# Turning activations by transfer instead of by matrix multiply: attention output and first expert tiles of a linear attention and mixture-of-experts kernel on one core

## Chip, core and metric

The kernel runs as one program on one core of a Trainium2 chip. The core's five engines work side by side and meet through semaphores: TensorE (PE; its weight loads are shown apart as PEld), VectorE (DVE), ScalarE (ACT), GpSimd (POOL) and SyncE (SP), which here only issues transfers. The metric is the device time of one execution in microseconds (us), the median over runs. A "turn" below is the transposition of a 128-row tile, so that its columns come to lie on the partitions and it can be the contracted operand of a matrix multiply.

## What is computed

Three stages follow one another: a linear attention with a decaying state over 4 x 8 heads of 768 steps and width 48; a dense two-layer block with a leaky ReLU; and a mixture of 8 experts, of which each token takes the one with the largest logit.

```python
# _attn_ref: per batch b, head h, step t
state = alpha[:, :, t, :, None] * state + np.einsum('bhd,bhe->bhde', k[:, :, t], v[:, :, t])
y[:, :, t] = np.einsum('bhd,bhde->bhe', q[:, :, t], state)
x = attn_out.transpose(0, 2, 1, 3).reshape(3072, 384)
# _moe_ref: w_in is 384 x 2048, w_out is 2048 x 384
h = x @ w_in
x = np.maximum(0.01 * h, h) @ w_out
# _moe2_ref: w1 is 8 x 384 x 1024, w2 is 8 x 1024 x 384
logits = x @ w_gate
expert_idx = np.argmax(logits, axis=1)
gate_w = softmax(logits)[np.arange(N), expert_idx]
for e in range(8):
    mask = expert_idx == e
    out[mask] = gate_w[mask, None] * (np.maximum(x[mask] @ w1[e], 0.0) @ w2[e])
```

## The kernel before

The 3072 tokens are worked in 8 **units** of 384 (NU = 8), each of three chunks of 128. Attention runs by chunks (scores, then the sum with the running state), with the decays folded into the keys and queries by VectorE scans. Precision is kept by splitting numbers into a float16 high and low part; each product is then three matrix multiplies (high-high, high-low, low-high).

**Attention's output** of a chunk is made in `chunk` (lines 693 to 789). The product stands in PSUM; VectorE finds its largest magnitude (L763) and a power of two (`pow2`, L537 to L542), ScalarE scales it into a float32 tile `xh` (L767), TensorE turns its three 128 x 128 blocks against an identity (L777 for units 2 to 7, L775 for units 0 and 1), ScalarE copies the turned high part to `xT` (L781) and VectorE subtracts to get the low part (L789). `xT` has two buffers.

**The dense block** is `moe1`: for each unit 16 groups of 9 multiplies against `w_in` (L825), whose results pass through `leaky` (ScalarE L802, VectorE L804, ScalarE L807, then GpSimd L809), and three sums of 48 multiplies against `w_out` (L834). `finish` scales the result to a float16 pair `xg` (L880 to L895). `route` computes logits, the chosen expert and each token's place in a list by experts in HBM (`x2s`), and GpSimd scatters the rows there (L967).

**The order** of all this is not written out: generators (`chunk`, `moe1`, `route` and so on) yield operations with an engine, an estimated duration, needs and rings of buffers, and the class `Loom` lists them by estimated start and by priority. The estimates set only the order. Transfers (engine "D") are issued on SP's queue, which works strictly in that order; low halves of weights are also loaded in between (`ck`, L531) and checked by VectorE (L533).

**The experts** work on 26 tiles of 128 gathered rows, four times (phases; each takes a quarter of the 1024 hidden columns). The first NA = 14 tiles hold full tiles of units 0 to 6, so that they can be gathered (`gather`, L1198, on GpSimd) while unit 7 is still in `moe1`. `tile_gathers` and `tile_turns` do as much of this as fits inside the Loom; `experts` goes on with the rest, one gather for each tile (L1490 ff.). `turn` transposes a gathered tile by six float16 blocks on TensorE (L1212), and a ScalarE copy (L1214) puts the result into `XT`. For each tile `experts` issues the 18 multiplies of `hidden` (L1334), the next gather, the copy of the expert's first weights (`stage`, L1251), ReLU parts (L1342, L1346), pieces of the next phase's weights, and the 6 multiplies of `combine` (L1363) of the tile two before. `last_tiles` runs beside the first tiles: the last unit's `route` with its three scatters, then `second_table`, then the 12 gathers of the remaining tiles. The expert number of a tile is read from `ej` into a register by `reg` (L1220) on VectorE, on TensorE and, for split tiles, on ScalarE; each read is followed by a check of its bounds.

## Time and profile before

| | us |
|---|---|
| median of 3 runs (768.33 to 771.94) | 769.94 |
| profiled execution, time | 772.55 |
| profiled execution, span from first to last instruction | 770.8 |
| TensorE busy in it (7927 multiplies) | 745.1 |
| VectorE / ScalarE / GpSimd busy | 607.2 / 483.0 / 378.7 |

Read the busy times against the span first, and then, stage by stage, which wait ends last on the engine that is busy nearly all the time; a timeline row shows in square brackets how long the engine sat idle before it and what released it. Matrix multiplies are pipelined and overlap in the rows, so the step from one start to the next, not the duration of a row, is what a multiply costs.

### The profile page before, as it was taken

What the parts mean: (1) busy time and instruction counts of PE and PEld (TensorE: products, weight loads), DVE (VectorE), ACT (ScalarE), POOL (GpSimd) and SP (SyncE); (2) the same over time, 40 slices, a digit from 0 to 9 for tenths busy, and PEclk for the clock granted to TensorE, in tenths of its full rate; (3) what the DMA queues carried; (4) which work ended last, traced back from release to release, by engine and by line L of the source; (5) the groups of instructions that cost most, each with busy time, mean ns of one, the idle gap of its engine ahead of it and who ended that gap; (6) DMA issues with size and microseconds to landing.
All of it is one profiled execution on the core that took longest, in us unless ns stands there. A gap on an engine that the chain in (4) does not pass through costs nothing.

```text
span 770.8 us, 21013 instructions
## 1 busy us (share of the span) xinstructions
PE 745.1 (97%) x7927; PEld 509.1 (66%) x7927; DVE 607.2 (79%) x1435; ACT 483.0 (63%) x1083; POOL 378.7 (49%) x406
## 2 busy tenths in 40 slices
PE   9999999998999999999999999899999999999994
PEld 4656675665666666656766665557777777777773
DVE  8999986599799879759855547756878899888673
ACT  4877576789866856845864645824676566667530
POOL 9135024451742763571581270553442588786543
PEclk9999999999999999999999999999999999999998
DMA  9914331153436234223001225224287555653341
GB/s 365 372 55 123 125 125 59 61 168 124 158 100 222 73 102 167 84 83 123 3 21 32 63 70 162 78 83 130 93 280 244 169 170 164 192 185 122 130 178 69
DMA packets 53131, 102.67 MB, mean 133 GB/s; under 512 B 4893, under 2 KB 37715, under 8 KB 53024
## 3 DMA queue, kind: packets, MB, share of 16 engines
q1 hardware_dynamic: 39360, 74.03, 29.9%
q0 software_dynamic: 4960, 14.62, 5.5%
q10 hardware_dynamic: 8704, 12.58, 4.8%
q8 instruction: 67, 1.10, 0.6%
q14 instruction: 40, 0.33, 0.1%
HBM read 79.17 MB, written 9.86 MB: 115 GB/s over the span
## 4 chain that ended last, share of the span: by engine, by line
PE 80%; DVE 11%; DMA 3%; issue 2%; ACT 2%; POOL 1%; ACTq 0%; DVEq 0%; POOLq 0%
PE m L834 22%; PE m L825 21%; PE a L1334 12%; PE m L1363 11%; PE a L710 3%; PE m L390 2%; PE a L754 2%; DMA wr<-in_moe_w 2%; PE a L669 1%; PE a L741 1%; PE a L637 1%; DVE st L1251 1%; DVE w L417 1%; DVE w L419 1%; PE a L486 1%
## 5 line engine op out<-in xcount | busy, mean ns | idle before, releaser
L834 PE MATMUL m<-woh,gh 128*128 128x392 f16 x1152 | 201.8, 329 | 0.0
L825 PE MATMUL m<-xT,wih 128*128 128x384 f16 x1152 | 193.8, 326 | 2.5 <-DVE gf L804 2.5
L809 POOL TENSOR_TENSOR gh<-gf,gh 128x384 f16<-128x384 f32 x128 | 119.0, 940 | 132.6 <-ACT gh L807 129.1
L825 PEld LDWEIGHTS <-wih 128*128 128x128 f16 x1152 | 111.8, 98 | 76.0 <-issue 4.7
L834 PEld LDWEIGHTS <-gh 128*128 128x128 f16 x1152 | 110.3, 98 | 73.4 <-issue 1.4
L1363 PE MATMUL m<-W,hs 128*128 (+1 forms) x624 | 119.1, 326 | 3.2 <-issue 1.8
L1334 PE MATMUL a<-XT,st 128*128 128x128 f16 (+1 forms) x1872 | 117.3, 215 | 3.0 <-DVE st L1251 1.6
L1334 PEld LDWEIGHTS <-st 128*128 128x128 f16 x1872 | 105.9, 98 | 21.0 <-issue 4.7
L804 DVE SCALAR_TENSOR_TENSOR gf<-m,gf 128x384 f32<-128x384 f32 x128 | 70.1, 554 | 55.6 <-ACT gf L802 55.4
L1251 DVE COPY st<-W 128x1536 f16 x104 | 82.7, 795 | 27.4 <-PE a L1334 16.2
L802 ACT ACTIVATE gf<-m 128x384 f32<-128x384 f32 x128 | 62.3, 489 | 42.9 <-PE m L825 39.1
L1342 ACT ACTIVATE hs<-a 128x256 f16<-128x256 f32 x104 | 39.7, 383 | 73.6 <-PE a L1334 52.8
L1363 PEld LDWEIGHTS <-hs 128*128 128x128 f16 (+1 forms) x720 | 57.6, 101 | 32.4 <-issue 3.0
L807 ACT CAST gh<-gf 128x384 f16<-128x384 f32 x128 | 64.4, 507 | 7.4 <-DVE gf L804 7.2
L1133 POOL TENSOR_TENSOR W<-wr,W 128x768 f16<-128x768 f32 x32 | 57.2, 1790 | 7.7 <-ACT W L1132 7.7
L1198 POOL DMA_INDIRECT acc<-x_rows,offj x26 | 30.3, 1164 | 37.3 <-DVE offj L1195 28.4
L1346 DVE SCALAR_TENSOR_TENSOR hs<-a,hs 128x256 f16<-128x256 f32 x104 | 43.2, 415 | 6.1 <-ACT hs L1342 5.4
L1106 POOL TENSOR_SCALAR wr<-wr 128x768 f32<-128x768 f32 x32 | 30.5, 952 | 27.7 <-DMA wr<-in_moe_w 14.9
L351 ACT ACTIVATE scrap<-W 128x768 bf16<-128x768 f16 x48 | 40.2, 838 | 5.9 <-ACT hs L1342 5.5
L1384 POOL DMA_INDIRECT out<-acc x26 | 26.5, 1019 | 31.7 <-DVE acc L1381 20.9
L967 POOL DMA_INDIRECT x_rows<-xg,pi x24 | 25.7, 1071 | 24.7 <-issue 6.4
L728 POOL TENSOR_TENSOR sh<-sm,sh 128x512 f16<-128x512 f32 x17 | 23.4, 1387 | 27.1 <-ACT sh L723 27.1
(279 smaller groups left out, 1238.6 us busy)
## 6 DMA issues: line engine op xcount, KB each, us to landing
wr<-in_moe_w SPq DMA_DIRECT2D x64, 384.0 KB
so<-W ACTq DMA_DIRECT2D x32, 384.0 KB
al<-in_aT SPq DMA_DIRECT2D x16, 390.0 KB
raw_in<-in_moe_w_in SPq DMA_DIRECT2D x12, 512.0 KB
kn__125<-in_kT SPq DMA_DIRECT2D x8, 768.0 KB
qn__126<-in_qT SPq DMA_DIRECT2D x8, 768.0 KB
raw<-in_moe_w_out SPq DMA_DIRECT2D x16, 384.0 KB
ck<-in_moe_w_in SPq DMA_DIRECT2D x24, 256.0 KB
```

Of the source, the lines that this page charges most:

```text
L351: A.activation(scrap, src, AF.Square, scale=scale, accum_out=g_sq[:, i : i + 1])
L802: A.activation(gf, ph[:, 0:UT], AF.Copy, scale=0.01 * CG)
L804: V.scalar_tensor_tensor(gf, ph[:, 0:UT], CG, gf, ALU.mult, ALU.max)
L807: A.copy(gh[:, 0], gf)
L809: E_[e].tensor_tensor(out=gh[:, 1], in0=gf, in1=gh[:, 0], op=ALU.subtract)
L825: T.matmul(ph[:, 0:UT], wih[:, a, kk, f * P : (f + 1) * P], xT[:, b, kk, :], start=(n == 0), stop=(n == 8),)
L834: T.matmul(po[:, 0:ROW], g[f][:, a, c * P : (c + 1) * P], woh_[0][:, b, f, :], start=(n == 0), stop=(n == 3 * NF - 1),)
L1133: G.tensor_tensor(out=lo, in0=raw, in1=hi, op=ALU.subtract)
L1251: V.tensor_copy(out=sth[i % 2].rearrange("p a k f -> p a (k f)"), in_=Wp[ph][0][:, :, ds(reg(V, j), 1), :, :].rearrange("p a e k f -> p a ...
L1334: T.matmul(hp[:, f * P + z * w : f * P + (z + 1) * w], st[z][:, a, kk, f * P : (f + 1) * P], XT[j][:, b, kk, z * w : (z + 1) * w], start=( ...
L1346: V.scalar_tensor_tensor(hs[:, 1].rearrange("p i t -> p (i t)"), hp[:, 0 : 2 * P], 0.0, hs[:, 0].rearrange("p i t -> p (i t)"), ALU.max, A ...
L1363: T.matmul(yp[z * w : (z + 1) * w, 0:DM], hs[:, a, i, z * w : (z + 1) * w], w2, start=(n == 0), stop=(n == 5), skip_group_check=True,)
```

## The change

Five things change.

- In `chunk`, units 2 to 7: ScalarE writes the scaled output as float16 (high part) straight into the first half of `xh`, VectorE writes the low part from PSUM into the second half (L772 of the new kernel), and one transfer on SP's queue (L778) turns all six blocks into `xT`. The three multiplies (L777), the copy (L781) and the subtraction (L789) of these 18 chunks go.
- `tile_turns` (L1250 of the new kernel) turns the tiles that are gathered inside the Loom by a transfer in place of six multiplies and a copy. In the built order these are five tiles; the other 21 are turned on TensorE as before.
- The last unit's scatters are declared free of the 14 first gathers (group "full"), so that they no longer wait for these to land.
- `experts` issues two first gathers instead of one in each of its first two tiles, and `last_tiles` loses one empty step.
- `reg` loads without the check of bounds.

Two estimates of the Loom change with it: when a buffer that a transfer reads comes free, and a lag in `route`; they only move the order.

```diff
         for name, key in op.free:
-            self.rings[name].drop(key, t)
+            self.rings[name].drop(key, t + (4.0 if last == "D" else 0.0))
...
+        if half:
+            yield O("A", 0.62)
+            x16 = pa.tile([P, DM], F32, tag="xh", name="xh", bufs=2).bitcast(F16)
+            A.activation(x16[:, 0:DM], yp[:, 0:DM], AF.Copy, scale=s1)
+            yield O("V", 0.62, free=[YA, ("n1", (u, c))])
+            V.scalar_tensor_tensor(
+                x16[:, DM : 2 * DM], yp[:, 0:DM], s1, x16[:, 0:DM], ALU.mult, ALU.subtract
+            )
+            yield O("D", 1.0, take=[("xT", u)], free=[("xh", (u, c))], post=[("xT", u, c)])
+            if r["xT"] is None:
+                r["xT"] = pm.tile([P, 2, 3, UT], F16, tag="xT", name="xT", bufs=2)
+            nc.sync.dma_start_transpose(out=r["xT"][:, :, :, sl].rearrange("p a k t -> p (a k) t"), in_=x16)
+            return
...
-                T.transpose(o, t, ident)
...
-            yield O("V", 0.58, free=[XA], post=[("xT", u, c)])
-            V.tensor_tensor(out=xT[:, 1, :, sl], in0=pxv, in1=xT[:, 0, :, sl], op=ALU.subtract)
...
-        yield O("v", 1.65, post=[("cu", u)], lag=1.0)
+        yield O("v", 1.65, post=[("cu", u)], lag=2.0 if u < NU - 2 else 1.0)
...
             tc.add_to_no_dep_group("list", sc.ins)
+            if last:
+                tc.declare_no_dep(sc.ins, group="full", reason="full tiles hold no row of the last unit")
...
+        if j < NA:
+            tc.add_to_no_dep_group("full", ga.ins)
...
-            regs[eng, j, z] = eng.value_load(ej[HALF * z : HALF * z + 1, j : j + 1], min_val=0, max_val=E - 1)
+            regs[eng, j, z] = nc.values_load(
+                ej[HALF * z : HALF * z + 1, j : j + 1], engines=(eng.engine,), min_val=0, max_val=E - 1,
+                skip_runtime_bounds_check_because="both tables hold 0 to E - 1 alone",
+            )
...
         for j in range(NA):
-            yield O("PA", (0.4, 0.75), need=[("acc", j)], take=[("a", ("t", j))], free=[("a", ("t", j))])
-            turn(j)()
+            yield O("D", 1.25, need=[("acc", j)])
+            nc.sync.dma_start_transpose(
+                out=XT[j].rearrange("p a k t -> p (a k) t"), in_=acc[j][:, 0:DM].bitcast(F16)
+            )
+            state["turned"] = j + 1
...
-        yield
         for j in order[0][NA:]:
...
-            next(firsts, None)
+            for _ in range(2 if i < 2 else 1):
+                next(firsts, None)
```

How the instructions stand differs at three places. The first is TensorE's queue ahead of unit 2, between the last chunk of that unit's attention (L754 ends its output) and the unit's first group of the dense block (L825; L833 in the new kernel). Before, what stood there in a row was:

```order
L834 LDWEIGHTS gh
L834 MATMUL m<-woh,gh 128x392
L637 MATMUL a<-ident,kt 128x128 x4
L669 MATMUL a<-vt,kn 64x48 x8
L777 MATMUL a<-ident,xh 128x128 x3
L710 MATMUL a<-qt,kt 64x128 x16
L825 LDWEIGHTS wih
L825 MATMUL m<-xT,wih 128x384
```

Now (`gh` is the dense block's hidden part, `wih` its first weights; the pair of L842 stands twelve times, as L834 is now numbered):

```order
L754 MATMUL a<-diag_111,qt 64x96 x8
L842 LDWEIGHTS gh
L842 MATMUL m<-woh,gh 128x392
...
L833 LDWEIGHTS wih
L833 MATMUL m<-xT,wih 128x384
```

The turn is gone, and the keys, sums and scores of unit 3 (L637, L669, L710) that stood beside it have moved behind the first 27 multiplies of unit 2.

The second is VectorE's queue at the same place, for the last chunk of unit 2, from the largest magnitude on. Before, from the unit's last `finish` on (the chunk's L763 stands four rows ahead):

```order
L880 TENSOR_REDUCE mx<-m 128x1
L537 TENSOR_SCALAR n2m<-mx 128x1
L541 TENSOR_SCALAR n2s<-n2m 128x1
L542 TENSOR_SCALAR n2e<-n2m 128x1
L882 TENSOR_SCALAR L<-m,n1e 128x8
L883 SCALAR_TENSOR_TENSOR gsc<-n1e,n2e 128x1
L614 SCALAR_TENSOR_TENSOR qt<-qn__126,R 128x12x64
L614 SCALAR_TENSOR_TENSOR qt<-qn__126,Ft 128x12x64
L895 SCALAR_TENSOR_TENSOR xg<-m,n2s,xg 128x384
L914 TENSOR_REDUCE rm<-L 128x3
L916 TENSOR_TENSOR rd<-L,rm 128x24
L789 TENSOR_TENSOR xT<-a,xT 128x3x128
```

Now, the whole way from L763 to the low part (L772):

```order
L763 TENSOR_REDUCE g_y<-a 128x1
L537 TENSOR_SCALAR n1m<-g_y 128x1
L541 TENSOR_SCALAR n1s<-n1m 128x1
L542 TENSOR_SCALAR n1e<-n1m 128x1
L614 SCALAR_TENSOR_TENSOR qt<-qn__126,R 128x12x64
L888 TENSOR_REDUCE mx<-m 128x1
L537 TENSOR_SCALAR n2m<-mx 128x1
L541 TENSOR_SCALAR n2s<-n2m 128x1
L542 TENSOR_SCALAR n2e<-n2m 128x1
L890 TENSOR_SCALAR L<-m,n1e 128x8
L891 SCALAR_TENSOR_TENSOR gsc<-n1e,n2e 128x1
L772 SCALAR_TENSOR_TENSOR xh<-a,n1s,xh 128x384
```

The low part comes ahead of one `qt` and of the dense block's `xg`, where the subtraction stood behind both.

The third is GpSimd's queue at the last unit's scatters (`x_rows`), with what each waits for (DMASW are the eight semaphores of GpSimd's own transfers). Before:

```order
L1198 DMA acc_6333<-x_rows,offj 128x386 [waits DMASW4_49,DVE_49]
L966 COPY xg<-con 128x1
L967 DMA x_rows<-xg,pi 32769x386 [waits DMASW3_49,DMASW2_49,DMASW4_49,DMASW1_49,DMASW5_49,DMASW0_49,DMASW6_49,DVE_49,DMASW7_49,Activation_49,Pool_49]
...
L1198 DMA acc_6334<-x_rows,offj 128x386 [waits DMASW6_49,DMASW7_49,DMASW5_49,DVE_49]
L1198 DMA acc_7973<-x_rows,offj 128x386 [waits DVE_49]
```

Now:

```order
L1208 DMA acc_6364<-x_rows,offj 128x386 [waits DMASW4_49,DVE_49]
L1208 DMA acc_6365<-x_rows,offj 128x386 [waits DMASW5_49,DVE_49]
L974 COPY xg<-con 128x1
L975 DMA x_rows<-xg,pi 32769x386 [waits DVE_49,DMASW6_49,Activation_49,Pool_49]
...
L1208 DMA acc_7747<-x_rows,offj 128x386 [waits DMASW6_49,DMASW1_49,DMASW7_49,DMASW0_49,DVE_49]
```

The 14th gather now stands ahead of the scatters instead of behind them, and a scatter waits for one earlier transfer on its semaphore instead of for all eight.

On SP's queue the 18 transfers of L778 stand among the loads of attention inputs and of `ck`, each behind the VectorE row that makes the low part; the five of L1250 stand one after another behind the last first-phase weight load and ahead of all 16 loads of the second phase's weights.

## Rows read from the trace of the kernel before

**Rows 1.** The page: busy time of each engine, then shares of the chain.

```profile
PE 745.1 (97%) x7927; PEld 509.1 (66%) x7927; DVE 607.2 (79%) x1435; ACT 483.0 (63%) x1083; POOL 378.7 (49%) x406
...
PE 80%; DVE 11%; DMA 3%; issue 2%; ACT 2%; POOL 1%; ACTq 0%; DVEq 0%; POOLq 0%
```

**Rows 2.** Groups by line and form: busy us, mean ns of one | idle.

```profile
L777 PE MATMUL a<-ident,xh 128*128 128x128 f32 x54 | 8.9, 277 | 0.4 <-ACT xh L767 0.4
...
L1212 PE MATMUL a<-ident,acc 128*128 128x128 f16 x156 | 13.0, 219 | 1.6 <-DMA acc<-x_rows,offj 1.6
```

**Rows 3.** Timeline, TensorE, 250 to 272: start us, busy us, instruction.

```profile
265.19 0.55 PE L777 MATMUL a<-ident,xh 128*128 128x128 f32 x3
...
265.57 4.55 PE L825 MATMUL m<-xT,wih 128*128 128x384 f16 x27
```

**Rows 4.** Timeline, TensorE, 515 to 575, end of unit 7, first tiles.

```profile
520.62 0.50 PE L1212 MATMUL a<-ident,acc 128*128 128x128 f16 x6
...
520.95 2.15 PE L834 MATMUL m<-woh,gh 128*128 128x392 f16 x12
...
530.75 2.17 PE L1334 MATMUL a<-XT,st 128*128 128x128 f16 x36
...
538.39 1.17 PE L1334 MATMUL a<-XT,st 128*128 128x128 f16 x18
```

**Rows 5.** Timeline of all engines, 164 to 192, start of unit 2.

```profile
179.11 0.88 PE L754 MATMUL a<-diag,qt 128*64 128x96 f32 x16
...
180.41 0.66 PE L834 MATMUL m<-woh,gh 128*128 128x392 f16 x3
...
181.52 0.55 DVE L763 TENSOR_REDUCE g_y<-a 128x1 f32<-128x384 f32 x1
...
183.05 0.67 PE L669 MATMUL a<-vt,kn 128*64 128x48 f32 x16 [1.54 <-issue]
...
183.52 0.95 DVE L614 SCALAR_TENSOR_TENSOR qt<-qn__126,R 128x768 f32<-128x768 f32 x1
...
185.26 0.61 DVE L895 SCALAR_TENSOR_TENSOR xg<-m,n2s,xg 128x384 f16<-128x384 f32 x1
...
185.40 1.10 PE L710 MATMUL a<-qt,kt 48*64 48x128 f32 x32 [1.20 <-DVE qt L614]
...
186.44 1.64 PE L825 MATMUL m<-xT,wih 128*128 128x384 f16 x9
```

**Rows 6.** Chain in order of time, 455 to 492: start, us, what.

```profile
467.91 5.82 DMA wr<-in_moe_w
...
484.14 3.13 DMA wr<-in_moe_w
```

**Rows 7.** Stretches: length, busy by engine, PEclk, DMA share, GB/s.

```profile
240.00:260.00 20.00, 20.00 (x202) 12.98 (x201) 19.24 (x48) 16.08 (x36) 10.20 (x10) 1.00 0.49 154
...
764.00:765.00 1.00, 0.00 (x0) 0.00 (x0) 0.00 (x0) 0.00 (x0) 0.69 (x2) 0.50 0.08 32
```

**Rows 8.** Timeline, GpSimd, 515 to 575, around the last unit's scatters.

```profile
541.59 1.09 POOL L1198 DMA_INDIRECT acc<-x_rows,offj  x1 [0.49 <-DVE hs L1346]
...
546.64 1.05 POOL L967 DMA_INDIRECT x_rows<-xg,pi  x1 [3.76 <-DVE hs L1346]
...
554.70 1.15 POOL L1198 DMA_INDIRECT acc<-x_rows,offj  x1 [3.79 <-DMA x_rows<-xg,pi]
```

**Rows 9.** Timeline, TensorE, 515 to 575, where the 14th tile is turned.

```profile
558.26 0.51 PE L1212 MATMUL a<-ident,acc 128*128 128x128 f16 x6 [1.62 <-DMA acc<-x_rows,offj]
```

**Rows 10.** Line 1220, register loads: engine, count, ns min/median/max.

```profile
L1220 DVEq FUSED_REGOPS  x26: 183/190/216, 512.5 to 590.3; - x26
...
L1220 PEldq FUSED_REGOPS  x26: 151/151/165, 534.4 to 599.2; - x26
```

**Rows 11.** Waits of TensorE: us in total, times, longest.

```profile
PE m L1363 <- issue: 1.8, 5, 0.4
```

**Rows 12.** Timeline, TensorE, 478 to 520, first layer of unit 7.

```profile
484.63 3.08 PE L825 MATMUL m<-xT,wih 128*128 128x384 f16 x18 [1.65 <-DVE gf L804]
```

More of the change, by code (lines that the diff above doesn't have):

```diff
@@ L764, in chunk @@
         s1, r["e1", c] = pow2(mx, K1, 1, "n1")
+        if "xT" not in r:
+            r["xT"] = None
+        if half:
[11 more added lines that the diff above has]
+            return
         yield O("A", 0.62, free=[YA, ("n1", (u, c))])
@@ L767, in chunk @@
         A.activation(xh, yp[:, 0:DM], AF.Copy, scale=s1)
-        yield O("P", 0.35 if u >= US else 0.68, take=[XA, ("xT", u)], free=[("xh", (u, c))])
-        if "xT" not in r:
+        yield O("P", 0.68, take=[XA, ("xT", u)], free=[("xh", (u, c))])
+        if r["xT"] is None:
             r["xT"] = pm.tile([P, 2, 3, UT], F16, tag="xT", name="xT", bufs=2)
@@ L773, in chunk @@
             t, o = xh[:, kk * P : (kk + 1) * P], px[:, kk * P : (kk + 1) * P]
-            if u < US:
-                T.matmul(o, t, ident, start=(kk == 0), stop=False, skip_group_check=True)
-            else:
-                T.transpose(o, t, ident)
+            T.matmul(o, t, ident, start=(kk == 0), stop=False, skip_group_check=True)
         pxv = px[:, 0:DM].rearrange("p (k t) -> p k t", k=3)
@@ L781, in chunk @@
         A.copy(xT[:, 0, :, sl], pxv)
-        if u < US:
-            yield O("P", 0.2)
-            T.matmul(pxv, idn16, xT[:, 0, :, sl], start=False, stop=True, skip_group_check=True)
-            yield O("A", 0.52, free=[XA], post=[("xT", u, c)])
-            A.copy(xT[:, 1, :, sl], pxv)
-        else:
-            yield O("V", 0.58, free=[XA], post=[("xT", u, c)])
-            V.tensor_tensor(out=xT[:, 1, :, sl], in0=pxv, in1=xT[:, 0, :, sl], op=ALU.subtract)
+        yield O("P", 0.2)
+        T.matmul(pxv, idn16, xT[:, 0, :, sl], start=False, stop=True, skip_group_check=True)
+        yield O("A", 0.52, free=[XA], post=[("xT", u, c)])
+        A.copy(xT[:, 1, :, sl], pxv)
     def scores_range(u, c, s_):
@@ L1197, in gather @@
     def gather(j):
-        G.indirect_dma_start(
+        ga = G.indirect_dma_start(
             out=acc[j].bitcast(I32),
```

## Prediction

> **What bounds the kernel now.** I read the page's busy times and chain first. TensorE is busy 745.1 us of a span of 770.8, and it makes 80% of the chain that ended last; VectorE makes 11% [rows 1]. So time taken out of TensorE's queue shortens the run, unless TensorE then waits at the same place for something else. Next I read TensorE's timeline at the three places where the change acts: the start of each unit that is turned, the passage from unit 7 to the expert tiles, and the tiles around the last unit's scatters. A row shows what TensorE does, the step to the next row what it costs, and the bracket what it waited for.
>
> **TensorE work removed.** The 54 multiplies of L777 come in 18 groups of three; their busy time of 8.9 us [rows 2] overlaps with neighbours. Their price is the step: 265.19 to 265.57, 0.38 us a group [rows 3]. 18 x 0.38 = 6.8 us. A gathered tile costs 520.62 to 520.95, 0.33 us [rows 4], and five of the 26 tiles go over to transfers: 5 x 0.33 = 1.65 us. Together 8.45 us. (All 156 multiplies of L1212 are 13.0 us busy [rows 2]; 126 of them stay.)
>
> **The wait added at unit 2.** A turn by transfer adds a wait: TensorE's first group of a unit waits until the third chunk's transfer has landed. Units 3 to 7 get their third chunk well ahead, since attention runs a unit ahead of the dense block and `xT` has two buffers. Unit 2 doesn't, because in the trace its dense block starts as soon as its scores and `xT` are there. The chunk's output ends at 179.11 + 0.88 = 179.99; until the first group at 186.44 TensorE does small work of unit 3 and idles 1.54 + 1.20 = 2.74 us [rows 5]. In the new order only twelve multiplies of the unit before stand there, about 2.0 us by the twelve at 520.95 [rows 4]; the work of unit 3 follows later and still has to be done. The way to the transfer is on VectorE: from the magnitude to the next large row 183.52 - 181.52 = 2.0 us (the same small rows stand between), one `qt` of 0.95, and the low part, which I take at 0.61 like `xg`, also float16 from PSUM [rows 5]; about 3.5 us. ScalarE's high part lies beside the `qt`. Call L the time from the end of the low part to landed data. Then TensorE idles 3.5 + L - 2.0 = 1.5 + L, against 2.74 before: L - 1.2 us more.
>
> No transposing transfer is in this trace, so L needs bounds. The nearest rows are weight loads on the same queue, counted from VectorE's release to the use: 3.13 us for one with little beside it, 5.82 for one behind others [rows 6]. These carry 128 x 768 float32 numbers, 384 KB, a turn 128 x 768 float16 numbers, 192 KB, but a turn writes columns of 2-byte numbers and stands behind `ck` loads. I take 5.0, nearer the loaded row, and keep 3.1 and twice the longest row, 11.6, as ends. With 5.0 the idle time is 6.5 us and the term is -3.8 us.
>
> A rule of the Trainium skill speaks against the change here: "VectorE: DVE Perf Modes", section "The three transpose paths", gives 390 ns for a 128 x 128 bf16 turn on TensorE and 1309 ns by transfer, and its rules advise TensorE wherever PSUM will do as the destination. By these figures six blocks one after another would be an estimated 7.9 us before landing. This case's trace has 0.38 us for three blocks on TensorE, well under 390 ns each, and no run so far shows the transfer.
>
> **The clock.** With nothing on TensorE for 6.5 us the granted clock may fall. It is 1.00 (2.4 GHz) in the stretch from 240 to 260, and 0.50 (1.2 GHz) from 764 to 765, just after TensorE's work ends [rows 7]. The shorter pauses of 1.54 and 1.20 us did not lower it visibly. The work right after the pause is 27 multiplies in a row, 4.55 us at the full clock [rows 3]; at half clock it would be 4.5 us more. I take -2 us, with ends 0 and -4.5.
>
> **The tiles turned by transfer.** Five transfers stand on SP's queue, each waiting for its gather. Behind them wait the 16 loads of the second phase's weights, whose first use is some nine tiles away; that hides them. (Two pieces more, 15 for 13, are finished beside the tiles, about 0.95 us each on VectorE; the checks it loses are 26 x 0.19 = 4.9 us [rows 10], so I cost this at nothing.) The fifth tile is the late one: its data is needed 538.39 - 530.75 = 7.6 us after the first tile's [rows 4]. If its gather lands about a microsecond after the first tile starts, L up to 6.5 is hidden, and each microsecond above it costs one.
>
> **Scatters and gathers.** The first scatter of unit 7 sat 3.76 us behind the gather of 541.59, and the 14th gather stood behind all three scatters until 554.70 [rows 8]. TensorE then waited 1.62 us for that tile [rows 9]. With the 14th gather ahead of the scatters and these free to go, that wait should vanish: +1.6 us, ends 0 and 1.6. The remaining 12 gathers need the scatters landed and come four tiles later, which covers them.
>
> **Registers.** Each checked load on TensorE has a 0.15 us bounds row [rows 10]. TensorE stood still five times before L1363 for 1.8 us in all [rows 11]; 5 x 0.15 gives +0.8 us, ends 0 and 1.8. The other checks lie behind multiplies.
>
> **Weights of the first phase.** At 484.63 TensorE waited 1.65 us for VectorE [rows 12], which then converted weights. The new order converts some of them later: +0.5 us, ends 0 and 1.65.
>
> **Edits at nothing.** ScalarE loses 18 copies and five of `XT`, VectorE swaps one row from PSUM for another; neither is waited for more. The two estimates move only the order. The empty step brings the last gathers one tile earlier.
>
> **Sum.** 8.45 - 3.8 - 2.0 + 0.5 + 0.8 + 1.6 = 5.5 us (5.55). The profiled execution took 772.55 us with a span of 770.8, so it would take 767.0. The median of the runs shown is 769.94, 2.6 lower, and I put the gain on that: 764.4 us. Written with L: gain = 12.6 - L - clock - (L - 6.5 where L is above that).
>
> **Rivals.**
>
> *Transfers as slow as twice the longest load.* L = 11.6. For it: the trace has no such transfer, and every other transfer of SP would also wait behind it. Against it: 192 KB is half of what landed in 3.13 us. The time: 12.6 - 11.6 - 2.0 - 5.1 = -6.1, so 776.0 us, slower. The gain is gone at L = 8.55, and the loss passes 3.85 us at 10.5. The page named above would place L near this end.
>
> *The freed time is refilled by VectorE.* In 240 to 260 VectorE is busy 19.24 of 20 us [rows 7]. If VectorE sets the pace of units 2 to 5, their turns come out of TensorE only to become waits for its rows, and 12 x 0.38 = 4.6 us of the gain go: 5.5 - 4.6 = 0.9, so 769.0 us, no change. Against it: TensorE shows 20.00 of 20 us busy in that stretch [rows 7], so it was not waiting there.
>
> *A quick transfer and no fall of the clock.* L = 3.1, clock 0: 12.6 - 3.1 = 9.5, so 760.4 us.
>
> That the change does not do what it says can be left out for the turns, since the built order shows them gone; only five of the tiles are covered, and the sum counts five.
>
> **How the numbers follow.** About 0.5%, 3.85 us, is what a measurement of this kernel can tell from no change. The forecast, L between 3.5 and 6.5 with some loss from the clock, gets 0.55, of which 0.05 ends within 0.5%. The quick transfer gets 0.05, the refill 0.22, the slow transfer 0.15, of which 0.03 is within 0.5% since L may lie below 10.5. The last 0.03 is a small loss or none, from reordered rows. So faster 0.55, same 0.30, slower 0.15. The range reaches from the quick transfer with all of the 1.65 us at 484.63 (another 1.15), 759, up to L near 10, with a gain of 12.6 - 10 - 2 - 3.5 = -2.9, 773. The slow end beyond it holds about 0.1, the quick end 0.05.
>
> **What would show it right or wrong.** Right: the first L833 of unit 2 starts about 9 us after L754 ends, with an idle bracket of 6 to 7 us; the starts of units 3 to 7 are then each about 1.1 us earlier against the one before; no bracket on the 14th tile; the first tile starts some 4 us earlier. The granted clock after the pause tells the clock's term. Wrong: an idle bracket at unit 2 above 10 us, brackets at the first L833 of units 3 to 7, brackets at tiles 3 to 5 for the transfers, or brackets of L833 for `gf` of VectorE in units 3 to 5 that add up to the turns taken out.

## The result and the profile of the changed kernel

The changed kernel takes 759.46 us, median of 5 runs (758.35 to 761.02), the kernel before beside it 768.58 us (768.0 to 771.94): a ratio of 0.988, interval 0.985 to 0.991. The gain is 9.1 us where 4.2 was forecast against the same yardstick (764.4 against 768.58) and 5.5 against the traced execution. The time lies inside the range. The profiled execution took 758.35 us. Its page gives the engines' busy time, and the waits of TensorE show what it stood still for (us in total, times, longest):

```profile
span 756.6 us, 20752 instructions
PE 736.5 (97%) x7843; PEld 501.3 (66%) x7843; DVE 606.8 (80%) x1429; ACT 475.6 (63%) x1063; POOL 382.9 (51%) x409
...
PE m L833 <- DMA xT<-xh: 4.6, 1, 4.6
PE m L833 <- DVE gf L812: 1.5, 2, 0.8
PE a L1352 <- ACT XT L1226: 1.1, 3, 0.8
...
PE m L1381 <- issue: 0.3, 1, 0.3
```

TensorE is busy 8.6 us less [rows 1] and has one new long wait, for the transfer at unit 2. The wait for the 14th tile [rows 9] is gone and the waits for issue [rows 11] fall from 1.8 to 0.3 us. (L833 is the first layer here, L842 the second, L1352 `hidden`, L1381 `combine`, L1224 the turn of a tile, L1226 its copy.)

Starts on TensorE in the two first traces:

| us | before | after | difference |
|---|---|---|---|
| unit 3, first group | 247.33 | 246.67 | 0.7 |
| unit 7, first group | 478.43 | 475.88 | 2.55 |
| first expert tile | 530.75 | 525.33 | 5.4 |
| 27th tile, where the second phase begins | 596.82 | 588.28 | 8.5 |
| end of the span | 770.8 | 756.6 | 14.2 |

From the 27th tile on, the queues of both kernels hold the same work; that the traces differ by another 5.7 us there is mostly not the change (see the trace c_before below).

The start of unit 2 in the timeline of the changed kernel, all engines:

```profile
175.88 0.88 PE L754 MATMUL a<-diag,qt 128*64 128x96 f32 x16
...
176.70 2.16 PE L842 MATMUL m<-woh,gh 128*128 128x392 f16 x12
176.81 0.56 DVE L763 TENSOR_REDUCE g_y<-a 128x1 f32<-128x384 f32 x1 [0.90 <-PE a L754]
...
180.02 0.62 DVE L772 SCALAR_TENSOR_TENSOR xh<-a,n1s,xh 128x384 f16<-128x384 f32 x1
...
180.66 1.22 SPq L778 DMA_TRANSPOSE xT<-xh  x1
...
183.48 7.39 PE L833 MATMUL m<-xT,wih 128*128 128x384 f16 x27 [4.61 <-DMA xT<-xh]
```

The low part ends at 180.64, the transfer is issued at 180.66, and the group that waits for it starts at 183.48: L is 2.84 us, not 5.0. TensorE idles 4.61 us, not 6.5, against 2.74 before [rows 5]. The 27 multiplies then take 7.39 us where they took 4.55 [rows 3], since the granted clock (the column behind the engines' busy times) has fallen during the pause and comes back only between 189 and 190:

```profile
182.00:183.00 1.00, 0.00 (x0) 0.00 (x0) 1.00 (x1) 0.84 (x4) 1.00 (x2) 0.71 0.93 175
...
184.00:185.00 1.00, 1.00 (x4) 0.45 (x3) 0.96 (x3) 0.19 (x2) 0.74 (x1) 0.50 0.69 135
...
190.00:192.00 2.00, 2.00 (x16) 1.40 (x14) 1.42 (x4) 1.22 (x3) 1.05 (x2) 1.00 0.66 240
```

### The profile page after: what moved, and what is told of

The parts are those of the page before. It is cut to its first block, busy times and chain, and to the rows that moved or that the text cites. A ratio compares the mean times of both kernels' runs of the same rounds, so it can differ in the third digit from the quotient of the medians.

```text
span 756.6 us, 20752 instructions
## 1 busy us (share of the span) xinstructions
PE 736.5 (97%) x7843; PEld 501.3 (66%) x7843; DVE 606.8 (80%) x1429; ACT 475.6 (63%) x1063; POOL 382.9 (51%) x409
## 5 line engine op out<-in xcount | busy, mean ns | idle before, releaser
L833 PE MATMUL m<-xT,wih 128*128 128x384 f16 x1152 | 196.8, 329 | 6.1 <-DMA xT<-xh 4.6
L842 PE MATMUL m<-woh,gh 128*128 128x392 f16 x1152 | 200.3, 329 | 0.0
L833 PEld LDWEIGHTS <-wih 128*128 128x128 f16 x1152 | 112.5, 99 | 81.3 <-issue 6.0
L842 PEld LDWEIGHTS <-gh 128*128 128x128 f16 x1152 | 110.2, 98 | 75.1 <-issue 1.5
L1381 PE MATMUL m<-W,hs 128*128 (+1 forms) x624 | 118.6, 327 | 0.5 <-issue 0.3
L1352 PEld LDWEIGHTS <-st 128*128 128x128 f16 x1872 | 106.1, 98 | 19.5 <-issue 2.9
L1352 PE MATMUL a<-XT,st 128*128 128x128 f16 (+1 forms) x1872 | 116.4, 215 | 2.1 <-ACT XT L1226 1.1
L812 DVE SCALAR_TENSOR_TENSOR gf<-m,gf 128x384 f32<-128x384 f32 x128 | 69.9, 553 | 56.1 <-ACT gf L810 55.8
L1269 DVE COPY st<-W 128x1536 f16 x104 | 80.0, 769 | 21.7 <-PE a L1352 19.7
L1381 PEld LDWEIGHTS <-hs 128*128 128x128 f16 (+1 forms) x720 | 57.3, 101 | 29.1 <-issue 1.2
L1143 POOL TENSOR_TENSOR W<-wr,W 128x768 f16<-128x768 f32 x32 | 58.8, 1840 | 5.7 <-ACT W L1142 5.7
## 6 DMA issues: line engine op xcount, KB each, us to landing
kn__125<-in_kT SPq DMA_DIRECT2D x8, 768.0 KB, 4.6
qn__126<-in_qT SPq DMA_DIRECT2D x8, 768.0 KB, 6.2
```

The source lines that it names most:

```text
L812: V.scalar_tensor_tensor(gf, ph[:, 0:UT], CG, gf, ALU.mult, ALU.max)
L833: T.matmul(ph[:, 0:UT], wih[:, a, kk, f * P : (f + 1) * P], xT[:, b, kk, :], start=(n == 0), stop=(n == 8),)
L842: T.matmul(po[:, 0:ROW], g[f][:, a, c * P : (c + 1) * P], woh_[0][:, b, f, :], start=(n == 0), stop=(n == 3 * NF - 1),)
L1143: G.tensor_tensor(out=lo, in0=raw, in1=hi, op=ALU.subtract)
L1269: V.tensor_copy(out=sth[i % 2].rearrange("p a k f -> p a (k f)"), in_=Wp[ph][0][:, :, ds(reg(V, j), 1), :, :].rearrange("p a e k f -> p a ...
L1352: T.matmul(hp[:, f * P + z * w : f * P + (z + 1) * w], st[z][:, a, kk, f * P : (f + 1) * P], XT[j][:, b, kk, z * w : (z + 1) * w], start=( ...
```

## Experiments on unit 2 and on attention's part

These four ran together on one chip (kernel before: 768.44 us). In the three variants the built order is kept; only the edited instructions are added or replaced.

The changed kernel again (c_after). 

> The changed kernel itself once more, beside the kernel before on the same chip, so that the variants sent with it have their own yardstick. Theory: the gain repeats, ratio 0.985 to 0.991 to the kernel before, and the starts of units and tiles repeat within 1 us against the first trace. Rival: part of the 9.1 us lay between chips or sessions, and the ratio is 0.992 or above.

Measured: 760.03 us, ratio 0.988 (0.985 to 0.991). The gain repeats, 8.4 us here.

TensorE kept busy in the pause (k_warm):

```diff
                 ph = pst("m")
+                if u == 2 and not f:
+                    for _ in range(17):
+                        T.matmul(
+                            ph.rearrange("p (a t) -> p a t", a=4), idle,
+                            idle.unsqueeze(1).to_broadcast([P, 4, P]), start=True, stop=True,
+                        )
```

Each of the 17 multiplies has 512 columns of zeros.

> The changed kernel with its built order kept to the row: 17 multiplies of zeros (512 columns each) are added on TensorE just ahead of the first group of unit 2, into the PSUM tile which that group then overwrites; nothing else moves. Theory: the earlier trial of this (u2_warm) did hold the clock, and lost the time again in the first expert tiles only because the planner's estimates, and with them the order there, changed. With the order kept the 27 multiplies take 4.6 us in place of 7.39, the units from 3 on start 2.8 us earlier than in c_after, the tiles too, and the time is 2 to 3 us below c_after. Rival: what is won at unit 2 is lost at the tiles in any order, since their first weights or gathers set the pace there; t0 comes 2.8 us earlier, the end does not, and the time is that of c_after within 0.7 us.

Measured: 757.17 us, ratio 0.984 (0.981 to 0.987), 2.9 us below c_after. The transfer still ends the wait, but the clock holds:

```profile
183.35 4.56 PE L839 MATMUL m<-xT,wih 128*128 128x384 f16 x27 [0.94 <-DMA xT<-xh]
...
187.00:188.00 1.00, 1.00 (x10) 0.74 (x9) 1.00 (x2) 0.99 (x4) 0.00 (x0) 1.00 0.96 303
```

Unit 3 starts at 243.71 against 246.88 in c_after, 3.2 us earlier, and unit 7 still 3.1 us earlier, so VectorE does not take it back. The six times spread widely (755.5 to 760.7 us against 758.8 to 762.0), so the size rests on the traces.

That size is not the same in every execution. Ten traces hold this pause, 4.61 or 4.62 us long. In four (after, c_after, k_regs, k_tiles_2) the granted clock then stays at 0.50 for 6.8 us, and the 27 multiplies take 6.93 to 7.49 us. In six (c_after_2, c_after_3, k_scat, k_tiles, k_regs_2, k_scat_2) it comes back after 3.4 us, and they take 5.94 to 6.24. The rows of c_after_3:

```profile
183.67 6.15 PE L833 MATMUL m<-xT,wih 128*128 128x384 f16 x27 [4.62 <-DMA xT<-xh]
...
184.00:185.00 1.00, 1.00 (x5) 0.48 (x4) 0.96 (x4) 0.00 (x0) 0.93 (x2) 0.50 0.26 55
...
187.00:188.00 1.00, 1.00 (x8) 0.59 (x6) 0.97 (x3) 0.92 (x3) 0.00 (x0) 1.00 1.02 379
```

Against the 4.56 us of k_warm the clock thus costs 1.4 to 2.9 us, for one and the same pause. What decides between the two is open.

One turn put back on TensorE (k_u2pe):

```diff
+            on_pe = (u, c) == (2, 2)
...
+            if on_pe:
+                px = pst("a")
+                for kk in range(3):
+                    T.transpose(px[:, kk * P : (kk + 1) * P], x32[:, kk * P : (kk + 1) * P], ident)
+                pxv = px[:, 0:DM].rearrange("p (k t) -> p k t", k=3)
+                A.copy(r["xT"][:, 0, :, sl], pxv)
+                V.tensor_tensor(out=r["xT"][:, 1, :, sl], in0=pxv, in1=r["xT"][:, 0, :, sl], op=ALU.subtract)
+                return
```

> The changed kernel with its built order kept: only the third chunk of unit 2 is turned on TensorE again (three multiplies, one copy, one subtraction at the place where its transfer stood). Theory: the wait for the transfer (4.61 us) goes and is replaced by one of 2 to 3 us for the subtraction; the clock stays at 1.00; the first group of unit 2 starts 1 to 2 us earlier than in c_after, unit 3 some 4 us earlier, and the time is 3 to 4.5 us below c_after. Rival 1: the subtraction comes late in VectorE's queue, the pause stays above 4 us and the clock falls as before; c_after within 1 us. Rival 2: as in the first trial (u2_pe) the tiles lose it; t0 3 to 4 us earlier, the end not.

Measured: 755.76 us, ratio 0.983 (0.980 to 0.986), 4.3 us below c_after, so faster than both kernels. The pause is 1.84 us, the clock holds, and unit 7 starts 2.7 us earlier than in c_after (473.35 against 476.06):

```profile
182.35 4.65 PE L844 MATMUL m<-xT,wih 128*128 128x384 f16 x27 [1.84 <-ACT xT L786]
```

The first tile starts 4.3 us earlier, but 1.6 us of that are a wait for `gf` in unit 7 that c_after has, and that lasts from nothing to 1.59 us in the traces of the changed kernel.

All of attention's turns back on TensorE (k_attn): the same edit with `on_pe = True`. 

> The changed kernel with its built order kept, but all 18 turns of attention's output on TensorE again, each at the place of its transfer; the other parts of the change stay. Theory: TensorE gets back 18 x 0.38 = 6.8 us and loses the pause's extra (1.9 us) and the clock's cost (2.8 us), so the time is 2.1 us above c_after (1 to 3.5), and the difference stands at the first group of unit 7. Rival: the turns also hold up other work by their place in the queues of ScalarE and VectorE, and the part is worth 5 to 9 us; then unit 7 starts 5 us or more later than in c_after. Second rival: VectorE paces the units anyway and the part is worth nothing; within 0.7 us of c_after.

Measured: 763.6 us, ratio 0.992 (0.988 to 0.994), 3.6 us above c_after; unit 7 starts at 478.91, 2.85 us later. From the start of unit 3 on, the distance to c_after grows from unit to unit by 1.0, 1.0, 1.5 and 0.3 us; the stretches hold 3, 3, 5 and 1 turns, so a turn costs 0.30 to 0.34 us, a little less than the 0.38 of the prediction. At unit 2 this variant pauses as well, and it too pays some clock, 6.02 us for the 27 multiplies:

```profile
182.61 6.02 PE L844 MATMUL m<-xT,wih 128*128 128x384 f16 x27 [2.01 <-ACT xT L786]
...
183.00:184.00 1.00, 1.00 (x5) 0.47 (x4) 1.00 (x3) 0.97 (x4) 1.00 (x2) 0.50 0.00 0
```

By the sizes measured in the first traces, attention's part is 6.84 - 1.87 - 2.84 = 2.1 us against the kernel before, whose clock held at 1.00. Against k_attn the longer pause (4.61 against 0.37 + 2.01) takes 2.23 and the clock 7.49 - 6.02 = 1.47 us, which leaves 6.84 - 2.23 - 1.47 = 3.1; unit 7 says 2.85 and the times 3.6. Since the clock's cost moves by 1.5 us from execution to execution, no closer agreement can be had. Held against k_u2pe, whose one turn is on TensorE, k_attn is 7.8 us slower: that is what the other 17 transfers bring.

## Experiments with parts of the change, the order free to move

These four ran together on another chip (kernel before: 773.71 us). Here the planner made a new order.

Attention's transfers alone, in the kernel before (e_attn: the chunk's hunk and the first estimate of the diff). 

> The kernel before with one part of the change: the attention output of units 2 to 7 turned by transfers (with the estimate of when their buffer comes free). Theory: this part is 6.8 us of multiplies taken out, less about 1.9 us of added pause and 2.8 us of clock at unit 2, so the first tile starts 2 to 3 us earlier than before and the time is 2 to 3 us below the kernel before, 765.5 to 766.6. Rival: the part carries most of the measured 9.1 us because it also frees VectorE's and ScalarE's queues in the units; 760 to 762. Second rival: VectorE refills the freed time, first tile where it was, 768.6.

Measured: 773.25 us, ratio 1.001 (0.998 to 1.003): no gain, where 2 to 3 us were forecast. The trace suggests why. Without the other estimate (the lag in `route`), the choice of experts of unit 1 (L949) stands ahead of unit 2's first group, and TensorE waits for it:

```profile
186.58 0.59 PE L949 MATMUL a<-oh,con 128*128 128x24 f32 x2 [5.04 <-DVE rex L943]
188.34 0.62 PE L950 MATMUL a<-rex,con 128*128 128x24 f32 x2 [1.16 <-DVE rex L945]
...
190.00:193.00 3.00, 3.00 (x11) 1.45 (x10) 1.47 (x6) 0.49 (x1) 1.05 (x1) 0.50 0.65 176
```

In the changed kernel these two stand behind the 27 multiplies and wait for nothing. The waits at unit 2 are 6.2 us here where the transfer's is 4.61 there, the granted clock stays low until 193 to 194, and unit 7 starts at 480.28 (475.88 in the first trace of after). I had costed this estimate at nothing, since it "only" moves the order. That it alone decides is not shown: no run adds the lag by itself.

Unchecked registers alone (e_regs). 

> The kernel before with one part of the change: registers for the expert numbers are loaded without the check of bounds. Theory: of the waits of L1363 for issue (1.8 us in five) about 1.5 go, as in the changed kernel (0.3 left); 767.1 us, the first tile where it was at 530.75. Rival: the checks on TensorE, VectorE and ScalarE delay each of the 26 tiles, so that they also carry what the sum did not find (about 2 us); 765 us. Second rival: nothing, since other waits end last; 768.6.

Measured: 771.74 us, ratio 0.998 (0.996 to 1.001). The 2 us are of the theory's size, and the interval reaches to nothing: unclear. The waits of combine for issue are 0.8 us in its trace, 1.8 in the first trace of before and 3.5 in c_before. This trace also shows something else. Ahead of unit 2 it has the two waits of the kernel before, 1.54 and 1.20 us [rows 5], and here the clock falls behind them, for 3.4 us; in the two traces of the kernel before it does not:

```profile
183.11 0.67 PE L669 MATMUL a<-vt,kn 128*64 128x48 f32 x16 [1.54 <-issue]
...
185.45 1.90 PE L710 MATMUL a<-qt,kt 48*64 48x128 f32 x32 [1.20 <-DVE qt L614]
...
186.00:188.00 2.00, 2.00 (x31) 1.33 (x24) 1.93 (x7) 1.79 (x5) 0.71 (x1) 0.50 0.78 181
```

The turn of unit 2's third chunk on TensorE (u2_pe), the edit of k_u2pe with estimates of its own. 

> The changed kernel with one turn put back: the third chunk of unit 2 is turned on TensorE as before, by three multiplies, a copy and a subtraction; the other 17 chunks stay with transfers. Theory: the pause of 4.61 us at the first group of unit 2 (L833 waits for the DMA of xT) and the fall of the clock behind it (27 multiplies in 7.39 us, against 4.55 in the kernel before) are what the transfer costs, about 1.9 us more idle time than before and 2.8 us of clock. With the turn on TensorE the bracket falls below 3 us, the 27 multiplies take about 4.6 us at a granted clock of 1.00, unit 3's first group comes 3 to 5 us earlier than in the changed kernel, and the time is 754.5 to 757. Rival: VectorE sets the pace of units 2 and 3, so that the time won comes back as waits of TensorE for gf or qt, and unit 3 starts where it did; 759.5 within 1 us.

Measured: 774.15 us, ratio 1.002 (0.999 to 1.004): far from the 754.5 to 757 of the theory. The bracket fell, to 2.31 us, but a second one of 1.42 us (for the subtraction) came behind three multiplies, and the granted clock was 0.50 for 6.8 us all the same:

```profile
182.65 1.00 PE L848 MATMUL m<-xT,wih 128*128 128x384 f16 x3 [2.31 <-ACT xT L778]
185.07 6.28 PE L848 MATMUL m<-xT,wih 128*128 128x384 f16 x24 [1.42 <-DVE xT L780]
...
188.00:189.00 1.00, 1.00 (x5) 0.48 (x4) 0.86 (x5) 0.62 (x2) 0.00 (x0) 0.50 0.93 301
```

Unit 3 starts at 247.42, later than in the first trace of after (246.67). The rest of the loss lies in the tiles.

Multiplies of zeros behind the transfer (u2_warm). 

> The changed kernel with 16 multiplies of zeros (512 columns each) set into TensorE's queue ahead of the first group of unit 2, where it stood idle for 4.61 us; they add nothing to any result. Theory: the pause itself stays, since the transfer's landing ends it (first group of unit 2 at about 183.5 us), but TensorE is busy in it, the granted clock stays at 1.00, and the 27 multiplies behind it take 4.6 us in place of 7.39: 2.8 us less, 756.6 us. Rival 1: the 27 multiplies are slow for another reason than the pause, such as contention from the transfers then running; they still take over 7 us and the time is 759.5. Rival 2: the clock holds but the time won is lost again to waits for VectorE in unit 2; first group of unit 3 no earlier, 759.5.

Measured: 766.87 us, ratio 0.990 (0.987 to 0.993). Unit 3 starts at 243.92 and the first tile at 521.41, as the theory had it, yet the stretch from the first to the 27th tile takes 72.3 us, where it took 62.95 in the first trace of after (596.82 - 530.75 = 66.1 before). In u2_pe it takes 74.4. I first put this down to the new order. The next section shows that such stretches come with the order unmoved, too.

## Experiments with the other parts, and what the chip does

On a third chip (kernel before: 772.55 us): the kernel before once more, and the changed kernel, order kept, with one part undone in each.

The kernel before (c_before). 

> The kernel before once more, for a second trace: the two profiled executions of before and after differ by 14.2 us where the medians differ by 9.1, so the first trace of before holds some 4 us that a usual execution does not. Theory: the starts of the units repeat within 1 us, and the 4 us lie in single waits of the expert tiles (1.62 us at the 14th tile, the waits at 629 to 636 and 716 to 729, the late relu at 760). Rival: those waits are all there again, and the profiled executions of this kernel are longer than the timed ones throughout.

Measured: one execution, 772.67 us. Its starts repeat the first trace of before, in the tiles too: 27th tile at 597.04 (596.82), last multiply at 763.17 (763.15), though single waits differ, and the first tile comes 1.4 us later. Neither theory nor rival holds as it was put. The 4 us do not lie in the single waits, and the profiled execution is not longer than the timed ones of its chip (median 772.55). What both traces of before share is the end: the stretch behind the 27th tile takes 166.1 us here and 166.3 in the first trace, against 161.1, 161.1 and 161.6 in the traces of the changed kernel whose chips run the kernel before in 768.4 to 768.6 us. On a chip that needs 771.9 for it, the changed kernel takes 165.9 (below). On c_before's own chip, two variants of the changed kernel (k_regs, k_scat) take about 165.5 us there. So about 5 of the 14.2 us between the two first traces go with the chip and not with the change. The kernel before was not traced on a chip of the quicker sort.

Checked registers again (k_regs: `eng.value_load(...)` as before). 

> The changed kernel with its built order kept, but the expert numbers loaded with the check of bounds, as before. Theory (the sum's term 0.8, up to 1.8): the waits of the second layer (combine) for issue come back, 1 to 2 us over the first 26 tiles, and the stretch from the first tile to the 27th is 1 to 2 us longer than in c_after (62.6 us); the time is 0.99 times the kernel before, 1 to 2 us above the changed kernel. Rival: the checks hold VectorE's and ScalarE's queues as well and cost 3 us or more. Second rival: nothing, within 0.5 us in that stretch.

Measured: 768.79 us, ratio 0.996 (0.993 to 0.998).

Scatters that wait for the first gathers, one gather a tile, the empty step back (k_scat). 

> The changed kernel with its built order of the units kept, but the last unit's scatters wait for all first gathers again, one first gather is issued per tile, and the empty step is back. Theory (the sum's term 1.6): the 14th gather stands behind the scatters again and TensorE waits at the 14th tile for about 1.6 us or more (more, since the tiles come earlier against GpSimd's queue); the stretch from the first tile to the 27th is 1.5 to 3 us longer than the 62.6 us of c_after. Rival: the 1.62 us of before were a chance of that execution, no bracket at the 14th tile, the stretch within 0.5 us.

Measured: 766.42 us, ratio 0.994 (0.992 to 0.996). The gather of the 14th tile stands behind the scatters again, yet no turn of a tile waits for its gather: the rival's point.

The five early tiles turned on TensorE (k_tiles: `turn(j)()` at the transfer's place). 

> The changed kernel with its built order kept, but the five tiles gathered ahead are turned on TensorE and copied by ScalarE, at the places of their transfers. Theory (the sum's term): 5 x 0.33 = 1.65 us more between unit 7's first group and the first tile (50.2 us in c_after), tiles from there on as in c_after; the time 1.5 to 2 us above the changed kernel, ratio to the kernel before about 0.990. Rival: the turns lie in waits of TensorE that are there anyway (it waits for the copied weights at the second and third tile), and the part is worth under 0.7 us. Second rival: with ScalarE's copies among the first relus the first tiles are held up more, 3 us.

Measured: 770.53 us, ratio 0.998 (0.996 to 1.000). Held against 0.988, the three parts would be worth 5.6, 4.2 and 7.8 us, more than the whole change. That comparison is between chips, so the three were run again beside the changed kernel, on a fourth chip (kernel before: 771.94 us).

The changed kernel (c_after_2). 

> The changed kernel once more, as the yardstick of the three variants sent with it, which before had none on their own chip. Theory: ratio to the kernel before 0.985 to 0.991 again. Rival: on a chip where the kernel before is slower (772 us and above) the changed kernel gains less, 0.991 to 0.996, and the parts taken out one by one would then each have looked too dear.

Measured: 770.0 us, ratio 0.996 (0.994 to 0.999). On this chip the change is worth 1.9 us, not 8.4. The variants:

> The changed kernel, order kept, with checked registers, now beside the changed kernel. Theory: 1 to 2 us above c_after_2, as the sum's term has it. Rival, by the first trial (0.9956 against 0.988): 4 to 6 us above, since in the new order each tile is turned only one tile ahead and every delay of the engines around it shows at TensorE as a wait for XT.

> The changed kernel, order kept, with the five early tiles turned on TensorE, now beside the changed kernel. Theory: 1.5 to 2.5 us above c_after_2 (five groups at 0.33 us, of which 1 to 1.7 us showed at the first tile). Rival, by the first trial (0.9984): 6 to 8 us above, because the copies of ScalarE hold up the first relus and tiles.

> The changed kernel, order of the units kept, with scatters that wait for the first gathers, now beside the changed kernel. Theory: 1 to 2 us above c_after_2 (the 1.62 us at the 14th tile, in other places, since the first trial showed no bracket there but waits for XT of ScalarE, 3.4 us in six). Rival: 4 us above.

Measured: checked registers 767.29 us, 0.993 (0.990 to 0.996); early tiles on TensorE 770.35 us, 0.997 (0.994 to 1.000); scatters that wait 765.95 us, 0.991 (0.987 to 0.994). None of the parts gains by its time on this chip, and two seem to cost: without the unchecked registers the kernel is 2.7 us faster than c_after_2, without the edits on scatters and gathers 4.1 us (five of its six times, 764.1 to 767.1, lie below all twelve of c_after_2, 767.4 to 773.3).

What the traces still say: from unit 7's first group to the first tile k_tiles_2 takes 49.54 us and c_after_2 48.12, and neither has an idle row of TensorE there; 1.4 us for the five turns, 1.65 in the sum. The registers' waits of combine for issue are 1.0 us in k_regs_2 and 0.8 in c_after_2.

Where does c_after_2 lose? Unit 7 starts at 476.60, as on the other chips. From the first to the 27th tile it takes 69.9 us (62.6 in c_after), and behind that 165.9 (161.1). One such place, the fourth and fifth tile, timeline:

```profile
529.96 1.18 PE L1352 MATMUL a<-XT,st 128*128 128x128 f16 x18 [0.30 <-issue]
...
532.26 0.32 PE L1381 MATMUL m<-W,hs 128*128 x1 [0.31 <-issue]
...
533.70 0.38 ACT L1360 ACTIVATE hs<-a 128x256 f16<-128x256 f32 x1 [4.57 <-PE m L1381]
533.70 0.56 DVE L1269 COPY st<-W 128x1536 f16 x1 [2.71 <-PE m L1381]
...
534.32 1.18 PE L1352 MATMUL a<-XT,st 128*128 128x128 f16 x18 [1.73 <-DVE st L1269]
```

The product that ScalarE's relu needs is there at 531.14, yet ScalarE and VectorE both go on at 533.70, in the same instant, after a break in TensorE's own row. u2_warm has the same break at the same tile (4.37 us from tile to tile, 4.36 here; 1.99 in c_after), and k_tiles and k_tiles_2 have one of 5.21 us a tile earlier. All four ran on chips on which the kernel before takes 771.9 us or more. GpSimd issues five gathers there in a row, 1.3 to 1.6 us apart, from the two first gathers a tile that the change brought. k_scat and k_scat_2, with one gather a tile, ran on two of these chips and have no break here (1.99 us). So the edit on the gathers is a likely cause of part of the loss on such chips. It is not shown alone, since k_scat undoes three edits at once, and on the quicker chips the same five gathers in c_after_3 go with 1.99 us. No row names what the engines waited for; this stays open.

## An experiment with the lead of the turns

The waits of TensorE for a turned tile, in c_after, c_after_2 and c_before, one row from each:

```profile
PE a L1352 <- ACT XT L1226: 0.9, 1, 0.9
...
PE a L1352 <- ACT XT L1226: 4.7, 9, 0.8
...
PE a L1334 <- ACT XT L1214: 0.7, 2, 0.4
```

Here the changed kernel has a weakness that I had not read in its order. Before, the sixth tile was turned behind the fourth tile's multiplies, two tiles ahead of its use; now it is turned behind the fifth's, one tile ahead. Relu and copy of ScalarE then lie between a turn and the very next tile, c_after:

```profile
549.58 0.50 PE L1224 MATMUL a<-ident,acc 128*128 128x128 f16 x6
549.78 0.38 ACT L1360 ACTIVATE hs<-a 128x256 f16<-128x256 f32 x1 [0.49 <-PE a L1352]
...
550.12 0.80 ACT L1226 COPY XT<-a 128x768 f16<-128x768 f16 x1
...
550.97 1.17 PE L1352 MATMUL a<-XT,st 128*128 128x128 f16 x18
```

The copy ends at 550.92 and the tile starts at 550.97. The step is 2.39 us, where it is 2.31 before (from 541.59 to 543.90), and a delay of ScalarE beyond 0.05 us delays TensorE. One number gives the lead back (k_both, which has the edit of k_u2pe too):

```diff
-AHEAD1 = 4
+AHEAD1 = 3
```

> The changed kernel with two edits: the third chunk of unit 2 is turned on TensorE again (as in k_u2pe), and the expert tiles are turned one tile earlier (AHEAD1 3 for 4, which moves one turn on TensorE ahead by one tile, so that a tile is turned two tiles before its use, as it was in the kernel before). Theory: in the changed kernel each turn is only one tile ahead, the step of a tile is 2.39 us against 2.31 because relu and copy of ScalarE end 0.05 us before the next tile starts, and every delay of ScalarE shows at TensorE: 0.9 us of waits for XT where the kernel before takes 768.4, 4.7 us in nine where it takes 772. With two tiles the step is 2.31, the waits for XT fall below 1.5 us, and the stretch from the first to the 27th tile is 2 us shorter than in c_after_3 where the kernel before takes 768, 4 to 6 us shorter where it takes 772; with the first edit's 4 us at the first tile the time is 5.5 to 7 us or 8 to 10 us below c_after_3. Rival 1: the earlier turns wait for their gathers, brackets on the turns and no gain in that stretch; 4 us below c_after_3. Rival 2: the delays at the tiles are TensorE's own and not ScalarE's, so that the stretch stays as long; 4 us below.

> The changed kernel as the yardstick of k_both. Theory: its ratio to the kernel before goes by the chip, 0.985 to 0.991 where the kernel before takes about 768.5, 0.993 to 0.998 where it takes 772 or more. Rival: 0.996 on the last chip was a chance, and it is 0.988 here whatever the kernel before takes.

Measured on a fifth chip (kernel before: 768.36 us): c_after_3 759.74 us, ratio 0.988 (0.985 to 0.991); k_both 755.38 us, ratio 0.982 (0.979 to 0.986), 4.4 us below it. In the trace the edit does what it should: the step is 2.31 us, k_both has no wait for XT in its list where c_after_3 has 2.4 us in two, and the stretch from the first to the 27th tile is 61.6 us, the shortest of all traces, against 65.9. But that 65.9 is long itself: c_after and the first trace of after, the same kernel, take 62.6 and 62.95, and k_u2pe 64.8. And k_u2pe was 4.3 us below its c_after without that edit, so by the times the lead brings nothing that can be told apart on these chips; the 5.5 to 7 us of the theory were not reached, which leaves the two rivals' 4. On the others, where it should bring most, it was not run.

## Why the prediction was right or wrong

**TensorE work removed: right.** Up to the first group of unit 7 the two first traces hold the same 4491 multiplies besides those of the turns. What the change gains there, 2.55 us, and what the longer pause (1.87) and the clock (2.84) take away add up to 7.3 us for the 54 multiplies, 6.84 in the sum. The sign I had named, 1.1 us more at each unit, holds for units 4 and 5 (1.07 and 0.87) and not for 6 and 7 (-0.05 and 0.00), because the new order moved other multiplies between the units. The five tiles show 1.4 of their 1.65 us in k_tiles_2 against c_after_2.

**The wait at unit 2: the mechanism right, the size off; this is the step that failed.** L, the time from the low part to landed data, had bounds of 3.13 and 5.82 us from loads on the same queue [rows 6], and I took 5.0, "nearer the loaded row". The turn landed in 2.84, below both; it was issued 0.02 us after the low part ended, with nothing ahead of it on its queue. So the term is 2.74 - 4.61 = -1.87 us in place of -3.8. The rest of its working held: VectorE's way took 3.9 us for 3.5, TensorE's twelve multiplies 2.1 for 2.0, and 3.9 + 2.84 - 2.1 is the pause. The unit's first group starts 6.7 us after L754 ends, not 9.

**The clock: right in kind; its size varies.** 7.39 - 4.55 = 2.84 us in the first trace of after against 2 in the sum; over ten traces with this pause 1.4 to 2.9. The two together make attention's part 2.1 us in place of 1.0, and 2.55 as read at unit 7.

**Tiles turned by transfer: right.** No bracket waits for them, though they landed 3.6 to 6.8 us after issue.

**First-phase weights: about right.** The 1.65 us [rows 12] became 0.84 in the first trace of after, 1.59 in c_after, behind them 0.41 for `rex`; c_after_2 has neither. So what is won there is chance. From unit 7 to the first tile the change brought 2.9 us in the first traces, forecast 1.65 + 0.5. Without the idle rows the stretch is 50.5 us before and 48.2 after, 2.3 us for the five turns.

**Scatters and gathers, registers: not separated, and the price of 1.6 us was wrong.** The bracket at the 14th tile went, as forecast, but c_before doesn't have it either, with the same queue, and k_scat and k_scat_2 don't get it back. So I had priced a chance wait of one execution. The waits for issue, too, are 1.8 us in one trace of before and 3.5 in six in the other. The tile stretch is 3.1 us shorter between the first traces, forecast 2.4, but c_after_3, the same kernel as after, would make it 0.1 (65.9 against 66.1), so that the agreement is luck. On the chips where the parts were taken out one by one, none showed a gain that can be trusted.

**The sum.** Up to the 27th tile: 2.55 + 2.87 + 3.12 = 8.5 us, forecast 1.04 + 2.15 + 2.4 = 5.6. So half of what was missing (1.5 of 2.9) lies in attention's part: L gives 1.9 and the turns 0.4 more than forecast, the clock takes 0.8 more. The rest is 0.7 us each in two stretches in which executions of one kernel differ by more (50.2, 49.45 and 49.0 us from unit 7 to the first tile; 62.6, 62.95 and 65.9 from there to the 27th). By the times, 4.9 us separate 4.2 and 9.1: 1.4 of them because the kernel before took 768.58 beside the changed one and not 769.94, the rest because the gain itself was put too low.

**The rivals.** The quick transfer came nearest in time, 760.4 us, and was half true: L was below its 3.1, but the clock fell, which it had excluded, so its number is partly luck. The slow transfer and the refill by VectorE fell: no group of units 3 to 6 waits for `gf`. The page of the Trainium skill named in the prediction ("VectorE: DVE Perf Modes", "The three transpose paths") would have put a transfer of six blocks at an estimated 7.9 us; the trace has 2.84. The advice in the rules of that page, to turn on TensorE, holds here at the one place where the result is needed at once, as k_u2pe shows (4.3 us), and not at the other 17 chunks (7.8 us, k_attn against k_u2pe).

**What I left out.** That a gain may depend on the chip: 8.4 to 9.1 us in three comparisons (kernel before at 768.4 to 768.6), 1.9 in a fourth (771.94). On that chip the forecast would have been too large, not too small; there is only one such comparison, so that the chip decides is likely and not shown. And that the new order cost the tiles their lead.

## What to carry to other kernels

A transposing transfer pays where its data is wanted later, and can cost twice where TensorE stands waiting for it: once for the wait and once more for the clock that falls in it. So try the one turn at such a place on TensorE. Read in the new order not only what is gone but how far ahead of its use each remaining step now stands, since a step one tile ahead leaves little room for delays. Do not price a wait that you have seen in one trace only; look for it in a second. Compare parts of a change only with the whole on the same chip.

## What the runs showed of the hardware

A transposing transfer of 128 x 768 float16 numbers holds its queue for 1.22 us and lands 2.8 us after issue:

```profile
L778 SPq DMA_TRANSPOSE xT<-xh x18: 1212/1217/1331, 166.5 to 430.5; - x18
...
DMA to landing us min/median/max: 2.7/2.8/3.9
```

The plain loads of `wr`, with twice the bytes, take 3.7 us in the median on the same queue; the five turns behind gathers take 4.9. An idle time of 4.61 us brought TensorE's clock to 0.50 (1.2 GHz) in all ten traces that hold it, for 3.4 us in six and for 6.8 us in four. Waits of 0.37 and 2.01 us around one short turn (k_attn) did so for 3.4 us, 2.31 and 1.42 us (u2_pe) for 6.8 us, while 1.84 us (k_u2pe) did not. Waits of 1.54 and 1.20 us did not in two traces of the kernel before, and did for 3.4 us in e_regs. So the length of a pause alone did not tell, in these traces, whether and for how long the clock falls. With multiplies of zeros in the pause it stayed at 1.00 (2.4 GHz) in k_warm and u2_warm. And the same instructions, from the 27th tile to the end, took 161.1 us on one chip and 165.9 on another.
